# Linear attention beside a gated SwiGLU: x transposed by DMA throughout, loads split over two queues, fixed PSUM banks

## The chip, the cores and the metric

The kernel runs on one core of one Trainium2 chip. The metric is device time in microseconds, lower is better. A core has five engines that run side by side: TensorE (PE: matmuls; its weight loads are listed as PEld), VectorE (DVE), ScalarE (ACT), GpSimd (POOL) and SyncE (SP). Transfers are issued by SP and by ACT, each in its own program order, and are carried out by 16 DMA engines.

## The reference

The input x has 2,048 tokens of width 512. Two blocks work on the same x, and a gate of each token mixes them:

```python
x = A_x
g = _sigmoid((x * gate_w).sum(-1, keepdims=True))
a = _A_ref(x, A_wqkv, A_wo)       # linear attention, 32 heads of 16
b = _B_ref(x, B_w1, B_w3, B_w2)   # (silu(x @ w1) * (x @ w3)) @ w2, hidden width 1376
return g * a + (1 - g) * b
```

In the attention block q, k and v are the three thirds of `x @ wqkv`; `phi(t) = where(t > 0, t + 1, exp(t)) + 1e-6` is applied to q and k. For each head `kv` is the sum over tokens of the outer product of phi(k) and v, and `z` the sum of phi(k); the output is `phi(q) @ kv / (phi(q) . z + 1e-6)`, multiplied by `wo`. Nothing is causal. All data are bf16.

## The kernel before

**Stages.** The 2,048 tokens are 16 token tiles of 128 (index t), the width 512 is 4 pieces of 128 (index kc). A matmul contracts over the 128 partitions, so x is needed twice in SBUF: `xT` (width on the partitions, tokens along the row) as operand of every projection and of the SwiGLU, and natural `xN` (tokens on the partitions).

- *First stage (L296 to L337).* For each t a `k_step` (four matmuls with `wk` into a PSUM bank, then `phi`: an exponential on ACT, two operations on DVE, result `pk`), a `q_step` (the same with `wq`, result kept in `pq`), and a `g_step`, which adds `xN` transposed times `pk` into four PSUM banks that stay allotted for all 16 tiles. v is never formed: the sums over tokens of x times phi(k) are multiplied by `wv` later (`kv_step`). POOL adds up `pk` in `zacc`.
- *Second stage (L398 to L419).* For each of four blocks of 512 tokens ten `glu_step`s (eight matmuls each with `w1` and `w3`), with `kv_step`, `m2_step`, the denominators and the remaining 96 hidden columns (`rem_step`) set between them, and four `out_step`s, which combine both blocks and store.

**What sets the order.** The order of the program text is the order on each engine; no planner moves anything. Waits between engines and on transfers are put in from the tiles that are read and written. In the order of instructions each transfer also waits for the landing of the eighth transfer before it, counted over both queues.

**The loads (L86 to L115).** SP issues `xN` tile 0, `wk` 1, `wk` 2, `xN` tile 2, then `wq` whole, then transposing transfers (`transpose=True`) that write `xT` from x in HBM for tokens 512 to 1,023 (four, one for each kc, L96), `xN` tiles 4 to 7 (L97), transposing transfers for tokens 1,024 to 2,047 (four, L99), the rest of `xN`, and all remaining weights. ACT issues `wk` 0, `xN` tile 1, `wk` 3 and `xN` tile 3, and then the table load for its exponential.

**The first 512 tokens.** The first four token tiles of `xT` are not loaded: `transpose_step` (L191) transposes natural x on TensorE by means of an identity matrix (`ident`, built on POOL, L70), into PSUM tiles `xTp`, and DVE copies them to `xT` (L197). Before this come ten small matmuls on a zeroed tile (`warm_step`, L199), and two more behind the first transposes; their result is used nowhere. The text at L298 to L308 weaves transposes, `k_step` 0 and 1 together; then k2, k3, q0, g0, q1, g1, and from t = 2 on q(t), k(t+2), g(t).

**PSUM.** There are eight banks. Products (k, q, gate, up, the remainder) rotate over a pool of four (`mm_tile`). The other four are first those of `xTp`, then the accumulators of `g_step`, then a rotation for the a and b products (`ab_tile`), as pools that are opened one after the other.

The code that the change touches:

Of the kernel before, what the change touches and what calls it, by code (L numbers as in the profile page):

```python
# [16 lines left out]
def kernel(  # L17
# [17 lines left out]
    nc = tc.nc  # L35
    P = nc.NUM_PARTITIONS
# [5 lines left out]
    KC = D // P  # L42
# [6 lines left out]
    F0 = FC * P  # L49
    HPC = P // Dh  # L50
    NR = 2 * FR + 1
    NPE = TPB

    x2d = A_x.flatten_outer_dims()
    out2d = out.flatten_outer_dims()
    x_r = x2d.rearrange("s (kc d) -> s kc d", d=P)
# [7 lines left out]
    psum = ctx.enter_context(tc.tile_pool(name="psum", bufs=4, space=bass.MemoryType.PSUM))  # L64
# [4 lines left out]
    ident = consts.tile([P, P], BF16, name="ident")  # L69
    make_identity(nc, ident[:])  # L70


    xN = consts.tile([P, NT, D], BF16, name="xN")
# [6 lines left out]
    w3 = consts.tile([P, KC, F0], BF16, name="w3")  # L80
    w2 = consts.tile([P, FC + 1, D], BF16, name="w2")
    xT = consts.tile([P, KC, S], BF16, name="xT")
    dq = nc.sync
    aq = nc.scalar
    k_cols = slice(D, 2 * D)
    dq.dma_start(out=xN[:, 0, :], in_=x_t[:, 0, :])  # L86
    aq.dma_start(out=wk[:, 0, :], in_=wqkv_r[:, 0, k_cols])
    dq.dma_start(out=wk[:, 1, :], in_=wqkv_r[:, 1, k_cols])  # L88
    aq.dma_start(out=xN[:, 1, :], in_=x_t[:, 1, :])
    dq.dma_start(out=wk[:, 2, :], in_=wqkv_r[:, 2, k_cols])  # L90
    aq.dma_start(out=wk[:, 3, :], in_=wqkv_r[:, 3, k_cols])
    dq.dma_start(out=xN[:, 2, :], in_=x_t[:, 2, :])
    aq.dma_start(out=xN[:, 3, :], in_=x_t[:, 3, :])
    dq.dma_start(out=wq[:], in_=wqkv_r[:, :, 0:D])
    for kc in range(KC):
        dq.dma_start(out=xT[:, kc, TB : 2 * TB], in_=x_r[TB : 2 * TB, kc, :], transpose=True)  # L96
    dq.dma_start(out=xN[:, 4:8, :], in_=x_t[:, 4:8, :])  # L97
    for kc in range(KC):
        dq.dma_start(out=xT[:, kc, 2 * TB : S], in_=x_r[2 * TB : S, kc, :], transpose=True)  # L99
# [50 lines left out]
    def project(t, w, name, between=None):  # L150
        ts = slice(t * P, (t + 1) * P)
        ps = mm_tile(name + "_ps")
        for kc in range(KC):
            nc.tensor.matmul(  # L154
                ps[:], lhsT=xT[:, kc, ts], rhs=w[:, kc, :],
                start=(kc == 0), stop=(kc == KC - 1),
            )
            if kc == 1 and between is not None:
                between()
        return ps  # L160

    def phi(ps, dst, name):
# [20 lines left out]
            )  # L183

    def k_step(t):
        k_phi(t, project(t, wk, "k"))

    def q_step(t):
        phi(project(t, wq, "q"), pq[:, t, :], "q")

    def transpose_step(t, pool):  # L191
        ps = pool.tile([P, KC, P], BF16, tag="xTp", name="xTp")
        for kc in range(KC):
            nc.tensor.transpose(  # L194
                out=ps[:, kc, :], in_=xN[:, t, kc * P : (kc + 1) * P], identity=ident[:]
            )
        nc.vector.tensor_copy(out=xT[:, :, t * P : (t + 1) * P], in_=ps[:])  # L197

    def warm_step(ps, n):  # L199
        for _ in range(n):  # L200
            nc.tensor.matmul(
                ps[:, 0:256], lhsT=warm[:, 0:P], rhs=warm[:], start=True, stop=True
            )


    def rem_step(tb):

        hr = hrem[tb % 2]
        for half in range(2):
            ps = psum.tile([P, 2, 256], FP32, tag="mm", name="r_ps")  # L210
# [26 lines left out]
        dq.dma_start(  # L237
            out=hT[tb][:, FC, :].rearrange("p (tt q) -> p tt q", q=P),
            in_=hr[:].rearrange("p tt f -> p (tt f)"), transpose=True,
        )  # L240

    def glu_step(tb, fc):
        fs = slice(fc * P, (fc + 1) * P)
        tok = slice(tb * TB, (tb + 1) * TB)
        g_ps = mm_tile("gate_ps")
# [5 lines left out]
        u_ps = mm_tile("up_ps")  # L251
# [43 lines left out]

    hT = {}  # L296
    hT[0] = work.tile([P, FC + 1, TB], BF16, tag="hT", name="hT")
    with tc.tile_pool(name="psumT", bufs=NPE, space=bass.MemoryType.PSUM) as psumT:  # L298
# [10 lines left out]
    with tc.tile_pool(name="psumG", bufs=KC, space=bass.MemoryType.PSUM) as psumG:  # L309
        g_acc = [psumG.tile([P, D], FP32, tag="G", name=f"g_acc{kc}") for kc in range(KC)]  # L310

        def g_step(t):
            for kc in range(KC):
                nc.tensor.matmul(  # L314
                    g_acc[kc][:], lhsT=xN[:, t, kc * P : (kc + 1) * P], rhs=pk[t][:],
                    start=(t == 0), stop=(t == NT - 1),
                )

        k_step(2)
        k_step(3)  # L320
        q_step(0)
        g_step(0)
        q_step(1)
        g_step(1)
        for t in range(2, NT):
            q_step(t)
            if t + 2 < NT:
                k_step(t + 2)
            g_step(t)
        z_ps = mm_tile("z_ps")  # L330
        nc.tensor.matmul(z_ps[:], lhsT=ones[:], rhs=zaccb[:], start=True, stop=True)
        nc.vector.tensor_copy(out=zb[:], in_=z_ps[:])  # L332
        for kc in range(KC):
            if kc % 2 == 0:
                nc.vector.tensor_copy(out=Gsb[:, kc, :], in_=g_acc[kc][:])
            else:
                nc.scalar.activation(out=Gsb[:, kc, :], in_=g_acc[kc][:], func=ACT.Copy)  # L337

    psum2 = ctx.enter_context(tc.tile_pool(name="psum2", bufs=4, space=bass.MemoryType.PSUM))

    def ab_tile(name):
        return psum2.tile([P, D], FP32, tag="ab", name=name)

    def kv_step():
        kv_ps = psum2.tile([P, KC, P], FP32, tag="ab", name="kv_ps")
        for c in range(KC):
            cs = slice(c * P, (c + 1) * P)
            for kc in range(KC):
# [2 lines left out]
                    start=(kc == 0), stop=(kc == KC - 1),  # L351
                )
        nc.vector.tensor_tensor(
            out=kvT[:], in0=kv_ps[:],
            in1=bmask[:].rearrange("p h d -> p (h d)")[:, None, :].to_broadcast([P, KC, P]),
            op=ALU.mult,
        )

    def m2_step():
        for c in range(KC):  # L360
            ps = ab_tile("m2_ps")
# [6 lines left out]
    def out_step(tb, tt):  # L368
        t = tb * TPB + tt
        ts = slice(t * P, (t + 1) * P)  # L370
        tl = slice(tt * P, (tt + 1) * P)
        a_ps = ab_tile("a_ps")
# [9 lines left out]
        w = D // pieces  # L382
        for i in range(pieces):
            cs = slice(i * w, (i + 1) * w)
            b_ps = ab_tile("b_ps")
# [64 lines left out]
```

## Time and profile before

| what | value |
|---|---|
| median of 3 runs | 181.54 us (180.47 to 181.67) |
| the profiled execution | 182.96 us |
| its span | 181.2 us |
| PE busy | 176.6 us, 97% of the span |
| DVE busy | 103.2 us, 57% |
| ACT busy | 61.8 us, 34% |
| POOL busy | 55.3 us, 31% |
| read from HBM | 8.42 MB |
| first stage, by the first gate_ps matmul | until 49.86 us |

The time is that of the whole program on the device; the span is the part that the profile shows, from its first to its last instruction, and all places in time below are us from the span's start. A group's busy time can hide in that of another engine: what sets the end is read from the chain of work that ended last, which is followed back from the last instruction. Matmuls are pipelined, so a matmul's own duration (379 ns for 512 columns) is longer than the distance from one to the next.

### The profile page before, as it was taken

To read this page: it belongs to the slowest core of one execution; us is meant where nothing else is said; L and a number is where in the kernel's file an instruction comes from. 1 tells how busy PE (TensorE), PEld (TensorE's weight loads), DVE (VectorE), ACT (ScalarE), POOL (GpSimd) and SP (SyncE) were. 2 spreads that over 40 slices of the span, in tenths; PEclk is the share of its full clock that TensorE was granted. 3 is DMA by queue.
4 is the path that set the end of the run, shared out by engine and by line. 5 is a ranking of instruction groups with operands and counts; after the bars stand their busy time and mean duration, and the time that the engine had idled before them with its cause. 6 is when DMAs were issued, how large, how long until landed. Compare 5 with 4: busy or idle time off the path is not lost.

```text
span 181.2 us, 2439 instructions
## 1 busy us (share of the span) xinstructions
PE 176.6 (97%) x876; PEld 84.8 (47%) x876; DVE 103.2 (57%) x196; ACT 61.8 (34%) x110; POOL 55.3 (31%) x60
## 2 busy tenths in 40 slices
PE   7999999999999999999999999999999999999993
PEld 4444444444445464454444455444445544444452
DVE  1279889889899773466534345653434565343222
ACT  2153443544472533132233313223331322333130
POOL 5035335453558540247400024640003442000000
PEclk9999999999999999999999999999999999999999
DMA  5999999900001203032300003430000342000011
GB/s 149 241 244 204 252 353 398 368 3 0 5 0 29 58 0 62 29 87 66 81 0 4 0 29 87 73 77 0 0 0 29 89 81 67 0 0 0 29 40 50
DMA packets 28108, 14.88 MB, mean 82 GB/s; under 512 B 19424, under 2 KB 27072, under 8 KB 28096
## 3 DMA queue, kind: packets, MB, share of 16 engines
q1 hardware_dynamic: 27520, 14.20, 29.7%
q10 hardware_dynamic: 576, 0.52, 0.9%
q8 instruction: 7, 0.11, 0.3%
q14 instruction: 5, 0.04, 0.1%
HBM read 8.42 MB, written 2.10 MB: 58 GB/s over the span
## 4 chain that ended last, share of the span: by engine, by line
PE 95%; DMA 3%; SPq 0%; DVE 0%; issue 0%
PE b_ps L388 21%; PE gate_ps L247 19%; PE up_ps L253 19%; PE k_ps L154 8%; PE a_ps L374 8%; PE g_acc L314 8%; PE q_ps L154 8%; PE r_ps L214 3%; DMA wk<-in_A_wqkv_dram 3%; PE kv_ps L349 0%; PE m_ps L362 0%; PE xTp L194 0%; DVE o L392 0%; SPq L88 0%; SPq L86 0%
## 5 line engine op out<-in xcount | busy, mean ns | idle before, releaser
L259 DVE TENSOR_TENSOR hT<-up_ps,sg 128x512 bf16<-128x512 f32 x40 | 27.2, 680 | 30.9 <-PE up_ps L253 30.9
L253 PE MATMUL up_ps<-xT,w 128*128 128x512 bf16 x160 | 41.1, 379 | 0.0
L247 PE MATMUL gate_ps<-xT,w 128*128 128x512 bf16 x160 | 41.1, 379 | 0.0
L388 PE MATMUL b_ps<-w,hT 128*128 128x512 bf16 (+3 forms) x187 | 40.7, 367 | 0.0
L258 ACT ACTIVATE sg<-gate_ps 128x512 bf16<-128x512 f32 x40 | 23.9, 597 | 46.9 <-PE gate_ps L247 46.9
L281 POOL TENSOR_TENSOR pqs<-pq,rden 128x512 bf16<-128x512 bf16 x16 | 16.9, 1055 | 65.0 <-issue 60.0
L392 DVE SCALAR_TENSOR_TENSOR o<-b_ps,omg_all,aga 128x512 bf16<-128x512 f32 (+1 forms) x17 | 12.2, 720 | 28.4 <-PE b_ps L388 28.4
L388 PEld LDWEIGHTS <-hT 128*128 128x128 bf16 (+1 forms) x187 | 18.3, 98 | 19.9
L253 PEld LDWEIGHTS <-w 128*128 128x128 bf16 x160 | 15.7, 98 | 18.9
L247 PEld LDWEIGHTS <-w 128*128 128x128 bf16 x160 | 15.6, 98 | 18.4
L181 POOL TENSOR_TENSOR zacc<-zacc,pk 128x512 f32<-128x512 f32 x14 | 16.3, 1162 | 18.4 <-DVE pk L169 18.2
L379 ACT ACTIVATE aga<-a_ps,g_all 128x512 f32<-128x512 f32 x16 | 11.0, 687 | 28.9 <-PE a_ps L374 28.9
L154 PEld LDWEIGHTS <-xT 128*128 128x128 bf16 x128 | 12.8, 101 | 15.6 <-issue 1.2
L266 POOL TENSOR_TENSOR pr<-pq,zb 128x512 f32<-128x512 bf16 x16 | 18.4, 1154 | 2.5 <-DVE zb L332 2.5
L154 PE MATMUL k_ps<-wk,xT 128*128 128x512 bf16 x64 | 18.4, 414 | 0.3 <-DMA wk<-in_A_wqkv_dram 0.2
L314 PE MATMUL g_acc<-pk,xN 128*128 128x512 bf16 x64 | 16.4, 379 | 0.0
L374 PE MATMUL a_ps<-M,pqT 128*128 128x512 bf16 x64 | 16.4, 378 | 0.0
L154 PE MATMUL q_ps<-wq,xT 128*128 128x512 bf16 x64 | 16.4, 379 | 0.0
L164 ACT ACTIVATE eq<-q_ps 128x512 bf16<-128x512 f32 x16 | 9.6, 598 | 17.2 <-PE q_ps L154 16.1
L164 ACT ACTIVATE ek<-k_ps 128x512 bf16<-128x512 f32 x16 | 9.6, 598 | 9.3 <-PE k_ps L154 9.3
L169 DVE SCALAR_TENSOR_TENSOR pk<-k_ps,emk 128x512 bf16<-128x512 f32 x16 | 11.1, 692 | 1.6
L169 DVE SCALAR_TENSOR_TENSOR pq<-q_ps,emq 128x512 bf16<-128x512 f32 x16 | 11.1, 692 | 0.5
(47 smaller groups left out, 96.7 us busy)
## 6 DMA issues: line engine op xcount, KB each, us to landing
w<-in_B_w_dram SPq DMA_DIRECT2D x3, 1280.0 KB, 8.5
out_dram<-o SPq DMA_DIRECT2D x15, 128.0 KB, 1.9
xN<-in_A_x_dram SPq DMA_DIRECT2D x3, 512.0 KB, 5.6
wq<-in_A_wqkv_dram SPq DMA_DIRECT2D x1, 512.0 KB, 5.3
wv<-in_A_wqkv_dram SPq DMA_DIRECT2D x1, 512.0 KB, 9.0
wo<-in_A_wo_dram SPq DMA_DIRECT2D x1, 512.0 KB, 9.5
wk<-in_A_wqkv_dram ACTq DMA_DIRECT2D x2, 128.0 KB, 3.8
xN<-in_A_x_dram SPq DMA_DIRECT2D x2, 128.0 KB, 3.7
```

What stands on the lines that cost most here:

```text
L154: nc.tensor.matmul(ps[:], lhsT=xT[:, kc, ts], rhs=w[:, kc, :], start=(kc == 0), stop=(kc == KC - 1),)
L164: nc.scalar.activation(out=e[:], in_=ps[:], func=ACT.Exp)
L169: nc.vector.scalar_tensor_tensor(out=dst, in0=ps[:], scalar=0.0, in1=em[:], op0=ALU.max, op1=ALU.add)
L247: nc.tensor.matmul(g_ps[:], lhsT=w1[:, kc, fs], rhs=xT[:, kc, tok], start=(kc == 0), stop=(kc == KC - 1),)
L253: nc.tensor.matmul(u_ps[:], lhsT=w3[:, kc, fs], rhs=xT[:, kc, tok], start=(kc == 0), stop=(kc == KC - 1),)
L258: nc.scalar.activation(out=sg[:], in_=g_ps[:], func=ACT.Silu)
L259: nc.vector.tensor_tensor(out=hT[tb][:, fc, :], in0=u_ps[:], in1=sg[:], op=ALU.mult)
L266: nc.gpsimd.tensor_tensor(out=pr[t][:], in0=pq[:, t, :], in1=zb[:], op=ALU.mult)
L281: nc.gpsimd.tensor_tensor(out=pqs[:].rearrange("p (h d) -> p h d", d=Dh), in0=pq[:, t, :].rearrange("p (h d) -> p h d", d=Dh), in1=rden[t] ...
L314: nc.tensor.matmul(g_acc[kc][:], lhsT=xN[:, t, kc * P : (kc + 1) * P], rhs=pk[t][:], start=(t == 0), stop=(t == NT - 1),)
L374: nc.tensor.matmul(a_ps[:], lhsT=pqT[:, c, ts], rhs=M2[:, c, :], start=(c == 0), stop=(c == KC - 1),)
L388: nc.tensor.matmul(b_ps[:, 0:w], lhsT=hT[tb][:n, fc, tl], rhs=w2[:n, fc, cs], start=(fc == 0), stop=(fc == FC),)
```

## The change

All of `xT` now comes from transposing transfers, one for each token tile of 128 with all four kc pieces in it, and all of them on SP, from its first instruction on; the natural tiles 4 to 7, 8 to 11 and 12 to 15 stand behind the transposes 5, 8 and 11. ACT issues `wk` (pieces 0, 1, then 2 and 3 as one), `wq` in two halves and natural tiles 0 to 3 as one transfer, and then runs an exponential on one column of the zeroed tile. `ident`, `transpose_step` and the weaving are gone; twelve of the small matmuls stand ahead of k0. The first steps run in the order k0, k1, q0, k2, q1, g0, k3, g1 and from t = 2 on as before. The PSUM pools become eight tiles that are allotted once: products rotate over banks 4 to 7, the accumulators and then the a and b products use banks 0 to 3.

```diff
-    dq.dma_start(out=xN[:, 0, :], in_=x_t[:, 0, :])
+    def load_xT(t):
+        ts = slice(t * P, (t + 1) * P)
+        dq.dma_start(out=xT[:, :, ts], in_=x2d[ts, :], transpose=True)
+
+    def load_xN(q, t0, t1):
+        q.dma_start(out=xN[:, t0:t1, :], in_=x_t[:, t0:t1, :])
+
     aq.dma_start(out=wk[:, 0, :], in_=wqkv_r[:, 0, k_cols])
-    dq.dma_start(out=wk[:, 1, :], in_=wqkv_r[:, 1, k_cols])
-    aq.dma_start(out=xN[:, 1, :], in_=x_t[:, 1, :])
-    dq.dma_start(out=wk[:, 2, :], in_=wqkv_r[:, 2, k_cols])
-    aq.dma_start(out=wk[:, 3, :], in_=wqkv_r[:, 3, k_cols])
-    dq.dma_start(out=xN[:, 2, :], in_=x_t[:, 2, :])
-    aq.dma_start(out=xN[:, 3, :], in_=x_t[:, 3, :])
-    dq.dma_start(out=wq[:], in_=wqkv_r[:, :, 0:D])
-    for kc in range(KC):
-        dq.dma_start(out=xT[:, kc, TB : 2 * TB], in_=x_r[TB : 2 * TB, kc, :], transpose=True)
-    dq.dma_start(out=xN[:, 4:8, :], in_=x_t[:, 4:8, :])
-    for kc in range(KC):
-        dq.dma_start(out=xT[:, kc, 2 * TB : S], in_=x_r[2 * TB : S, kc, :], transpose=True)
-    dq.dma_start(out=xN[:, 8:12, :], in_=x_t[:, 8:12, :])
-    dq.dma_start(out=xN[:, 12:16, :], in_=x_t[:, 12:16, :])
+    aq.dma_start(out=wk[:, 1, :], in_=wqkv_r[:, 1, k_cols])
+    aq.dma_start(out=wk[:, 2:4, :], in_=wqkv_r[:, 2:4, k_cols])
+    aq.dma_start(out=wq[:, 0:2, :], in_=wqkv_r[:, 0:2, 0:D])
+    aq.dma_start(out=wq[:, 2:4, :], in_=wqkv_r[:, 2:4, 0:D])
+    load_xN(aq, 0, 4)
+    nc.scalar.activation(out=act_pre[:], in_=warm[:, 0:1], func=ACT.Exp)
+    for t in range(NT):
+        load_xT(t)
+        if t in (5, 8, 11):
+            i = {5: 4, 8: 8, 11: 12}[t]
+            load_xN(dq, i, i + 4)
...
-    def mm_tile(name):
-        return psum.tile([P, D], FP32, tag="mm", name=name)
+    bank = [psum.tile([P, D], FP32, name=f"bank{i}") for i in range(8)]
+    turn = {"mm": 0, "ab": 0}
+
+    def mm_tile():
+        turn["mm"] += 1
+        return bank[4 + (turn["mm"] - 1) % 4]
+
+    def ab_tile():
+        turn["ab"] += 1
+        return bank[(turn["ab"] - 1) % 4]
...
-        w_ps = mm_tile("warm_ps")
-        warm_step(w_ps, 10)
-        transpose_step(0, psumT)
-        warm_step(w_ps, 2)
-        k0 = project(0, wk, "k", between=lambda: transpose_step(1, psumT))
-        transpose_step(2, psumT)
-        k1 = project(1, wk, "k")
-        transpose_step(3, psumT)
-        k_phi(0, k0)
-        k_phi(1, k1)
...
-        k_step(2)
-        k_step(3)
-        q_step(0)
-        g_step(0)
-        q_step(1)
-        g_step(1)
...
+    for _ in range(12):
+        nc.tensor.matmul(
+            bank[3][:, 0:256], lhsT=warm[:, 0:P], rhs=warm[:], start=True, stop=True
+        )
+    k_step(0)
+    k_step(1)
+    q_step(0)
+    k_step(2)
+    q_step(1)
+    g_step(0)
+    k_step(3)
+    g_step(1)
+    for t in range(2, NT):
+        q_step(t)
+        if t + 2 < NT:
+            k_step(t + 2)
+        g_step(t)
```

More of the change, by code (lines that the diff above doesn't have):

```diff
@@ L6 @@
 from concourse._compat import with_exitstack
-from concourse.masks import make_identity
 ACT = mybir.ActivationFunctionType
@@ L51 @@
     NR = 2 * FR + 1
-    NPE = TPB
     x2d = A_x.flatten_outer_dims()
     out2d = out.flatten_outer_dims()
-    x_r = x2d.rearrange("s (kc d) -> s kc d", d=P)
     x_t = x2d.rearrange("(t p) d -> p t d", p=P)
@@ L63 @@
     work = ctx.enter_context(tc.tile_pool(name="work", bufs=2))
-    psum = ctx.enter_context(tc.tile_pool(name="psum", bufs=4, space=bass.MemoryType.PSUM))
+    psum = ctx.enter_context(tc.tile_pool(name="psum", bufs=1, space=bass.MemoryType.PSUM))
     ctx.enter_context(tc.manual_schedule())
@@ L68 @@
     nc.vector.memset(warm[:], 0.0)
-    ident = consts.tile([P, P], BF16, name="ident")
-    make_identity(nc, ident[:])
     xN = consts.tile([P, NT, D], BF16, name="xN")
@@ L82 @@
     xT = consts.tile([P, KC, S], BF16, name="xT")
+    act_pre = consts.tile([P, 1], BF16, name="act_pre")
     dq = nc.sync
@@ L144, with project @@
     th_all = consts.tile([P, NT], FP32, name="th_all")
-    def mm_tile(name):
-        return psum.tile([P, D], FP32, tag="mm", name=name)
-    def project(t, w, name, between=None):
-        ts = slice(t * P, (t + 1) * P)
-        ps = mm_tile(name + "_ps")
+    bank = [psum.tile([P, D], FP32, name=f"bank{i}") for i in range(8)]
[6 more added lines that the diff above has]
+        return bank[(turn["ab"] - 1) % 4]
+    def project(t, w):
+        ps = mm_tile()
         for kc in range(KC):
             nc.tensor.matmul(
-                ps[:], lhsT=xT[:, kc, ts], rhs=w[:, kc, :],
+                ps[:], lhsT=xT[:, kc, t * P : (t + 1) * P], rhs=w[:, kc, :],
                 start=(kc == 0), stop=(kc == KC - 1),
             )
-            if kc == 1 and between is not None:
-                between()
         return ps
@@ L185, in k_step, with g_step @@
     def k_step(t):
-        k_phi(t, project(t, wk, "k"))
+        k_phi(t, project(t, wk))
     def q_step(t):
-        phi(project(t, wq, "q"), pq[:, t, :], "q")
-    def transpose_step(t, pool):
-        ps = pool.tile([P, KC, P], BF16, tag="xTp", name="xTp")
+        phi(project(t, wq), pq[:, t, :], "q")
+    def g_step(t):
         for kc in range(KC):
[L194 to L200, printed above, removed]
             nc.tensor.matmul(
-                ps[:, 0:256], lhsT=warm[:, 0:P], rhs=warm[:], start=True, stop=True
+                bank[kc][:], lhsT=xN[:, t, kc * P : (kc + 1) * P], rhs=pk[t][:],
+                start=(t == 0), stop=(t == NT - 1),
             )
@@ L209, in rem_step @@
         for half in range(2):
-            ps = psum.tile([P, 2, 256], FP32, tag="mm", name="r_ps")
+            ps = mm_tile()[:].rearrange("p (j n) -> p j n", j=2)
             for j in range(2):
@@ L244, in glu_step @@
         tok = slice(tb * TB, (tb + 1) * TB)
-        g_ps = mm_tile("gate_ps")
+        g_ps = mm_tile()
         for kc in range(KC):
@@ L250, in glu_step @@
             )
-        u_ps = mm_tile("up_ps")
+        u_ps = mm_tile()
         for kc in range(KC):
@@ L297 @@
     hT[0] = work.tile([P, FC + 1, TB], BF16, tag="hT", name="hT")
-    with tc.tile_pool(name="psumT", bufs=NPE, space=bass.MemoryType.PSUM) as psumT:
-        w_ps = mm_tile("warm_ps")
-        warm_step(w_ps, 10)
-        transpose_step(0, psumT)
-        warm_step(w_ps, 2)
-        k0 = project(0, wk, "k", between=lambda: transpose_step(1, psumT))
-        transpose_step(2, psumT)
-        k1 = project(1, wk, "k")
-        transpose_step(3, psumT)
-        k_phi(0, k0)
-        k_phi(1, k1)
@@ L309 @@
[L309 to L317, printed above, removed]
-        k_step(2)
-        k_step(3)
-        q_step(0)
-        g_step(0)
-        q_step(1)
-        g_step(1)
[L325 to L337, printed above, removed]
@@ L339 @@
-    psum2 = ctx.enter_context(tc.tile_pool(name="psum2", bufs=4, space=bass.MemoryType.PSUM))
-    def ab_tile(name):
-        return psum2.tile([P, D], FP32, tag="ab", name=name)
+    for _ in range(12):
[15 more added lines that the diff above has]
+        g_step(t)
@@ L344, in kv_step @@
+    z_ps = mm_tile()
+    nc.tensor.matmul(z_ps[:], lhsT=ones[:], rhs=zaccb[:], start=True, stop=True)
+    nc.vector.tensor_copy(out=zb[:], in_=z_ps[:])
+    for kc in range(KC):
+        if kc % 2 == 0:
+            nc.vector.tensor_copy(out=Gsb[:, kc, :], in_=bank[kc][:])
+        else:
+            nc.scalar.activation(out=Gsb[:, kc, :], in_=bank[kc][:], func=ACT.Copy)
     def kv_step():
-        kv_ps = psum2.tile([P, KC, P], FP32, tag="ab", name="kv_ps")
+        kv_ps = ab_tile()[:].rearrange("p (c q) -> p c q", q=P)
@@ L353, in kv_step @@
         nc.vector.tensor_tensor(
-            out=kvT[:], in0=kv_ps[:],
+            out=kvT[:], in0=kv_ps,
             in1=bmask[:].rearrange("p h d -> p (h d)")[:, None, :].to_broadcast([P, KC, P]),
@@ L360, in m2_step @@
         for c in range(KC):
-            ps = ab_tile("m2_ps")
+            ps = ab_tile()
             nc.tensor.matmul(ps[:], lhsT=kvT[:, c, :], rhs=wo[:, c, :], start=True, stop=True)
@@ L371, in out_step @@
         tl = slice(tt * P, (tt + 1) * P)
-        a_ps = ab_tile("a_ps")
+        a_ps = ab_tile()
         for c in range(KC):
@@ L384, in out_step @@
             cs = slice(i * w, (i + 1) * w)
-            b_ps = ab_tile("b_ps")
+            b_ps = ab_tile()
             for fc in range(FC + 1):
```

## The prediction

> **What bounds the kernel now.** I read the page's chain that ended last first, then the same chain over the first 30 us, the DMA issues, and the SP queue in order of time.
>
> ```profile
> PE 95%; DMA 3%; SPq 0%; DVE 0%; issue 0%
> ```
>
> ```profile
> xN<-in_A_x_dram SPq DMA_DIRECT2D x3, 512.0 KB, 5.6
> wq<-in_A_wqkv_dram SPq DMA_DIRECT2D x1, 512.0 KB, 5.3
> ...
> pqT<-pqs SPq DMA_TRANSPOSE x16, 2.4
> ...
> xT<-in_A_x_dram SPq DMA_TRANSPOSE x8, 4.1
> ```
>
> TensorE carries 95% of the chain and one load the rest. So only a gap on PE, or PE work removed, moves the end; what other engines gain is worth nothing unless PE waits for them. The second fence is the DMA view; its last two figures are size and median us from issue to landing (a transpose has no size shown).
>
> The chain at the start (start us, us, what):
>
> ```profile
> 1.74 4.54 DMA wk<-in_A_wqkv_dram
> 6.28 0.04 issue
> 6.32 1.01 PE k_ps L154 x2
> 7.33 0.43 PE xTp L194 x4
> 7.76 1.71 PE k_ps L154 x4
> 9.46 0.43 PE xTp L194 x4
> 9.89 1.93 PE k_ps L154 x8
> 11.82 0.86 PE q_ps L154 x4
> 12.68 0.86 PE g_acc L314 x4
> ```
>
> Here the reader sees three things. The third quarter of wk lands at 6.28 and starts the chain. Four 512-column matmuls take 1.71 us at 7.76 but 0.86 us from 11.82 on: PE runs at half pace until about 10.1 (eight at 9.89 take 1.93, so one or two are slow). The granted-clock column says 1.00 throughout, so the pace has to be read from the matmuls. Two groups of transposes stand in the chain after 6.32, 0.43 us each. From 11.82 to 49.86, where gate_ps begins, PE has no gap.
>
> A "step" below is one k, q or g step (4 matmuls). **The yardstick:** before, six steps (k0 to k3, q0, g0) are through at 12.68 + 0.86 = 13.55 us. In the changed order the first six are k0, k1, q0, k2, q1, g0; the seventh and eighth are again the same set. So the change is worth the time at which its g0 ends, less 13.55, if nothing stalls later.
>
> **Part 1, removed.** Sixteen TensorE transposes and four DVE copies (425 ns each). On the chain the transposes are 2 x 0.43 = 0.86 us; the others ran while PE waited for wk. The DVE copies lay on a DVE that waited for them anyway: no gain by themselves.
>
> **Part 2, the transposing DMAs.** The SP queue in order of time prices the issues:
>
> ```profile
> 3.70 0.39 SPq L94 DMA_DIRECT2D wq<-in_A_wqkv_dram  x1
> 4.13 5.15 SPq L96 DMA_TRANSPOSE xT<-in_A_x_dram  x4
> 9.33 0.58 SPq L97 DMA_DIRECT2D xN<-in_A_x_dram  x1
> 9.96 5.88 SPq L99 DMA_TRANSPOSE xT<-in_A_x_dram  x4
> ```
>
> An issue takes some 1.25 us whether it carries 512 or 1,024 tokens (medians 1.256 and 1.297), and the 128-token pqT form takes 1.19. So SP goes from 8 transposing issues to 16, one token tile each 1.25 us: tile t is issued at about 0.8 + 1.25t, plus 0.55 for each natural load between. Landing took 3.0 to 5.4 us, median 4.1. PE takes a new tile each 2.6 us, so later tiles get ever more lead (tile 4: issued 5.8, landed by 11.2, needed about 16). Everything behind on SP moves: 16 x 1.25 + 3 x 0.55 ends at 22.5 instead of 17.06, 5.4 us later. w1 is then issued near 26 and, with the longest landing of a large weight (12.2), is in by 38; gate_ps needs it at 49.9. wv lands near 37 for 55.0, w2 near 42 for 71.1. Cost nothing, covered by 12 us and more.
>
> Natural tiles 4 to 7: issued near 8.3, in by 14.6 at 6.3 us; g4 comes near 22. Nothing.
>
> **Part 3, the ACT queue.** It now issues wk0, wk1, wk2:4 (quarters 2 and 3), wq0:2, wq2:4, xN0:4 (natural x, token tiles 0 to 3), and behind these stand the table load (1.28 us) and every exponential. The order of instructions shows that a DMA waits until the eighth DMA before it, over both queues, has landed: wq2:4 waits for xT1, xN0:4 for xT2. This is the new wait.
>
> - wk2:4: the old third quarter, issued at 1.74 (this one at about 1.73), landed at 6.28. Less lies ahead of it (two quarters on its own queue, about two transposes beside it). Bounds 5.0 (the 2.8 to 3.0 us of the first loads, on 256 KB) and 6.3; I take 6.0.
> - xT2 is issued at 3.3, lands by the median at 7.4 (6.3 to 8.7). xN0:4, 512 KB: 4.0, 5.6 and 6.3 us in three natural loads, 5.3 for wq. wq is nearest, as it went out into the same crowd. Landed at 7.4 + 5.3 = 12.7 (10.3 to 15.0).
> - wq2:4 goes out when xT1 lands, 2.05 + 3.5 = 5.5, and takes 2.7 (128 KB) to 5.3 (512 KB): 8.2 to 10.8, I take 9.5.
> - ACT is free for k0 at 7.4 + 0.45 issue + 1.28 table + 0.1 = 9.2; exponential 0.60, DVE 0.28 + 0.69: pk0 at 10.8. q1 wants its PSUM bank, and g0 wants it as operand.
>
> PE then: k0's second half 6.0 to 6.85, k1 to 8.56 (1.71), q0's first half to 9.41, its second waits to 9.5 and ends near 10.3, k2 11.2, q1 12.1. g0 could start at 12.1, but its weights are natural x, landed 12.7. Four matmuls in a row of their own take 1.03: 13.73 against 13.55. **Sum: +0.2 us.** The 0.86 saved and the earlier wk are handed back by waiting for the natural tiles, which earlier PE transposes needed at once and which now come last.
>
> A check by bytes: in half-us windows the old kernel has moved 2.13 MB by 11.0, which is wk, wq, xN0:4 (12 units of 131 KB), almost all of four transposed units, and table and code. The new one needs those 12, xT0 to xT5 and part of xN4:8: 18 to 20 units and table and code (0.15 MB), 0.38 to 0.64 MB more: at the 310 GB/s of 11 to 13 us by 12.2 to 13.1, at the 201 GB/s of 7.5 to 10.5 (transposes in flight) by 12.9 to 14.2. Both ends go into the range. A lone transpose (pqT) is seen here, columns from the left us, PE, weights, DVE, ACT, POOL, clock, DMA share, GB/s:
>
> ```profile
> 152.00:152.50 0.50, 0.50 (x4) 0.26 (x3) 0.07 (x1) 0.33 (x1) 0.00 (x0) 1.00 0.44 88
> 152.50:153.00 0.50, 0.50 (x4) 0.20 (x3) 0.00 (x0) 0.27 (x1) 0.00 (x0) 1.00 0.88 174
> ```
>
> It fills all DMA engines for 0.66 us (0.22 + 0.44) per 131 KB: 198 GB/s. The Trainium skill, "DMA: Bandwidth & Descriptors", section Latency and other measured facts, gives 261 GB/s for a DMA transpose; by that estimate six tiles cost 3.0 us of the engines and not 4.0, and natural x would land up to 1 us sooner. The row here is slower than the page.
>
> **Part 4, banks and the rest.** Products rotate over four banks and accumulators or a/b over four, as the pools did: from the eighth step on, each step still takes the bank of the one four before it. Nothing either way. The identity on POOL goes (nobody waits), the early exponential only fixes where the table load stands. From 13.7 on all rows repeat. DVE, busy 0.88 to 0.97 of the time from 10 us on, has no more to do than before.
>
> The profiled execution took 182.96 us, span 181.2 and 1.8 around it; with +0.2 it would be 183.2. The median of the runs, 181.54, lies 0.8% below it; applied there: **181.7 us**.
>
> **Rivals.**
>
> A. *PE, not natural x, is last.* xN0:4 lands before PE gets there (xT2 after 3.0 us, then 4.0: 10.3). g0 starts at 12.1, or with wk2:4 at 5.0 and no break at 11.5: 0.6 to 1.2 us earlier than 12.68. 180.3 to 180.9. For it: the faster windows (361 GB/s at 2.5 to 3.5). Against: between 7 and 10 us the DMA share reads above 1 in five of six half-us windows, transposes in flight, at 130 to 313 GB/s: the load is limited by the DMA engines there.
>
> B. *The slow pace lasts longer.* Before, PE was busy without a break from 6.32 until the pace doubled at 10.1, 3.8 us; it did not double after the broken stretch 1.1 to 6.3. If the break at wq2:4 (up to 10) starts this anew, PE stays slow to 13.8: k1 8.56, q0 10.4, k2 12.1, q1 13.8, g0 ends 14.8, +1.3: 182.8. The Trainium skill, "TensorE: Matmul & The Clock Gate", Part 1, has a free-running window of about 3.4 us that must be busy before full clock; by that page a miss costs an estimated 1.7 us. The 3.8 us here agrees with it roughly.
>
> C. *Slower: the ACT queue is held by landing transposes.* If transposes among copies land late (xT2 after 5.4: 8.7) and natural x at 6.3, g0 starts at 15.0: +2.5 us, 184.0; at the 128 GB/s seen in 8 to 9 us, the 1.15 MB that are left at 7.5 (2.64 less 1.50) take 8.9 us, 16.4 and +3.9, 185.4. ACT starts later as well (pk0 12.1, q1 stalls), but that lies inside. It decides from a landing at about 14.3, +1.8. For it: those two windows, and a queue that stands still behind each wait. Against: SP offers a 0.66 us transpose only each 1.25 us.
>
> **How the numbers follow.** Chances: forecast 0.40 (181.2 to 182.4), A 0.25, B 0.20, C 0.15. A measurement of this kernel tells about 1% (1.8 us) from no change: faster means under 179.7, slower over 183.4. A's 0.25 holds 0.08 past its best (the pace doubling early as well): faster. Slower: C and B's late part, 0.18. Same 0.74. The range reaches from A's low end to C's first price: 180.2 to 184.0.
>
> **What would show it.** Right: xTp gone, chain of the start going through the xN load of the ACT queue, g0 starting near 12.7, gate_ps at 50 +- 0.5, and matmul rows after that unchanged. A: g0 near 12 with no DMA in the chain but wk. B: 0.43 us matmuls after 11 us. C: a PE gap of over 1.5 us before g0, ACT idle before its table load. I am wrong altogether if a gap stands after 16 us: then the weights pushed back on SP, or the banks, cost what I put at nothing.

## The result, and the profile after

The changed kernel takes **187.08 us** (median of 4 runs, 186.54 to 187.45) against 181.41 beside it: a ratio of 1.0308, 95% interval 1.0283 to 1.0333. It is 5.7 us slower; the prediction was 181.7 us, range 180.2 to 184.0, with 0.18 on slower. Times here and below are medians of fast runs; the one slow run of a variant, 186.41 us of the kernel with the copies behind, is also the run that its trace shows.

The page's chain that ended last, after:

```profile
PE 91%; DMA 5%; SPq 1%; issue 1%; DVE 0%
```

PE's share of the chain fell from 95% to 91%, and two loads stand in it in place of one. The chain at the start (start us, us, what) shows which:

```profile
2.14 5.92 DMA xT<-in_A_x_dram
8.06 0.02 issue
8.08 4.02 DMA wq<-in_A_wqkv_dram
12.10 0.04 issue
12.14 4.11 PE bank L161 x10
16.24 0.86 PE bank L198 x4
```

The second transposing transfer (xT1, issued at 2.14) lands at 8.06. At 8.08 starts the load of wq's second half, which waited for it (by the order of instructions, xT1 is the eighth transfer before it), and lands at 12.10. Ten matmuls then take 4.11 us; at the pace of the next line (4 in 0.86) they would take 2.15. g0 ends at 17.11.

PE in order of time, after (start us, us, engine, line, what, idle before and what ended it):

```profile
6.02 1.01 PE L161 MATMUL bank<-wk,xT 128*128 128x512 bf16 x2 [0.34 <-DMA wk<-in_A_wqkv_dram]
8.10 1.89 PE L161 MATMUL bank<-wk,xT 128*128 128x512 bf16 x4 [1.07 <-DMA xT<-in_A_x_dram]
9.78 1.06 PE L161 MATMUL bank<-wq,xT 128*128 128x512 bf16 x2
12.14 1.01 PE L161 MATMUL bank<-wq,xT 128*128 128x512 bf16 x2 [1.29 <-DMA wq<-in_A_wqkv_dram]
12.94 1.91 PE L161 MATMUL bank<-wk,xT 128*128 128x512 bf16 x4
14.65 1.59 PE L161 MATMUL bank<-wq,xT 128*128 128x512 bf16 x4
16.08 1.03 PE L198 MATMUL bank<-pk,xN 128*128 128x512 bf16 x4
```

Read it in two ways. The brackets are the waits: for xT1 ahead of k1, and for wq in the middle of q0. The durations are the pace: four matmuls take 1.9 us up to k2 (0.43 from one to the next, and the last one's tail), 1.59 in q1, and 1.03 (0.22 from one to the next) only from 16 us on.

ACT in order of time, after:

```profile
2.20 0.67 ACTq L93 DMA_DIRECT2D wq<-in_A_wqkv_dram  x1
8.08 0.38 ACTq L94 DMA_DIRECT2D wq<-in_A_wqkv_dram  x1
8.49 0.48 ACTq L88 DMA_DIRECT2D xN<-in_A_x_dram  x1
9.01 1.28 ACT L96 ACT_TABLE_LOAD   x1 [9.01 <-DMA xT<-in_A_x_dram]
```

ACT stands still from 2.87 to 8.08, on the wait for xT1.

From g0 on nothing is new: gate_ps starts at 53.44 instead of 49.86, which is 3.58 later, as g0 ended 3.56 later (17.11 for 13.55), and the profiled spans differ by 3.4 (184.6 and 181.2). But the medians differ by 5.7. So the first question was where the other 2.2 us are.

### The profile page after: what moved, and what is told of

Read it like the earlier page. It is cut to its first block, busy times and chain, and to the rows that moved or that the text cites. A ratio compares the mean times of both kernels' runs of the same rounds, so it can differ in the third digit from the quotient of the medians.

```text
span 184.6 us, 2395 instructions
## 1 busy us (share of the span) xinstructions
PE 176.2 (95%) x844; PEld 83.5 (45%) x860; DVE 102.4 (55%) x192; ACT 61.8 (33%) x111; POOL 54.9 (30%) x58
## 4 chain that ended last, share of the span: by engine, by line
PE 91%; DMA 5%; SPq 1%; issue 1%; DVE 0%
PE bank L366 21%; PE bank L245 19%; PE bank L251 18%; PE bank L161 15%; PE bank L198 8%; PE bank L352 7%; DMA xT<-in_A_x_dram 3%; PE bank L212 3%; DMA wq<-in_A_wqkv_dram 2%; SPq L85 1%; PE bank L327 0%; PE bank L340 0%; DVE o L370 0%; PE bank L314 0%
## 5 line engine op out<-in xcount | busy, mean ns | idle before, releaser
L257 DVE TENSOR_TENSOR hT<-bank,sg 128x512 bf16<-128x512 f32 x40 | 27.2, 681 | 30.9 <-PE bank L251 27.8
L245 PE MATMUL bank<-xT,w 128*128 128x512 bf16 x159 | 41.0, 379 | 0.2
L366 PE MATMUL bank<-w,hT 128*128 128x512 bf16 (+3 forms) x186 | 40.6, 367 | 0.1
L251 PE MATMUL bank<-xT,w 128*128 128x512 bf16 x153 | 40.2, 379 | 0.2
L256 ACT ACTIVATE sg<-bank 128x512 bf16<-128x512 f32 x40 | 23.9, 597 | 46.9 <-PE bank L245 46.9
L370 DVE SCALAR_TENSOR_TENSOR o<-bank,omg_all,aga 128x512 bf16<-128x512 f32 (+1 forms) x17 | 12.2, 719 | 28.4 <-PE bank L366 28.4
L161 PE MATMUL bank<-wk,xT 128*128 128x512 bf16 x62 | 18.9, 427 | 2.2 <-DMA xT<-in_A_x_dram 1.9
L161 PE MATMUL bank<-wq,xT 128*128 128x512 bf16 x63 | 17.8, 405 | 1.3 <-DMA wq<-in_A_wqkv_dram 1.3
L198 PE MATMUL bank<-pk,xN 128*128 128x512 bf16 x63 | 16.4, 379 | 0.2
L352 PE MATMUL bank<-M,pqT 128*128 128x512 bf16 x61 | 16.3, 378 | 0.2
L174 DVE SCALAR_TENSOR_TENSOR pk<-bank,emk 128x512 bf16<-128x512 f32 x16 | 11.1, 692 | 2.0 <-PE bank L161 0.5
```

The lines of the kernel that those rows point to most:

```text
L161: nc.tensor.matmul(ps[:], lhsT=xT[:, kc, t * P : (t + 1) * P], rhs=w[:, kc, :], start=(kc == 0), stop=(kc == KC - 1),)
L198: nc.tensor.matmul(bank[kc][:], lhsT=xN[:, t, kc * P : (kc + 1) * P], rhs=pk[t][:], start=(t == 0), stop=(t == NT - 1),)
L245: nc.tensor.matmul(g_ps[:], lhsT=w1[:, kc, fs], rhs=xT[:, kc, tok], start=(kc == 0), stop=(kc == KC - 1),)
L251: nc.tensor.matmul(u_ps[:], lhsT=w3[:, kc, fs], rhs=xT[:, kc, tok], start=(kc == 0), stop=(kc == KC - 1),)
L256: nc.scalar.activation(out=sg[:], in_=g_ps[:], func=ACT.Silu)
L257: nc.vector.tensor_tensor(out=hT[tb][:, fc, :], in0=u_ps[:], in1=sg[:], op=ALU.mult)
```

## The experiments

Theory at this point: the loss lies in the first 16 us and has three parts, a landing (xT1), a wait on the ACT queue (wq's second half behind xT1) and the slow matmul pace, which the gaps prolong. Rivals: the banks, the 128-token transposes or the later weights cost something; or the DMA engines are simply full.

**The kernel before again** (no edit).

> The kernel before, unchanged, with a trace of its own. The median moved by 5.7 us, the two profiled spans by 3.4 (181.2 to 184.6). Theory: the profiled execution of before was a late one, in which the matmul pace doubled only at 10.1 us; other executions double earlier, have spans near 179.5, and this trace shows the pace doubling before 9 us. Rival: spans are again near 181.2 and the 2.2 us lie outside the span, so that the changed kernel loses time before its first or after its last instruction.

181.41 us, the same time. Its trace is another than that of the page before: the span is 179.6, and the ten spans of this set are 179.1 to 179.7. The chain at its start:

```profile
2.19 4.82 DMA xN<-in_A_x_dram
7.01 0.05 issue
7.05 0.40 PE xTp L194 x4
7.45 0.86 PE k_ps L154 x4
8.31 0.22 PE xTp L194 x4
8.54 1.73 PE k_ps L154 x8
10.26 0.86 PE q_ps L154 x4
11.13 0.86 PE g_acc L314 x4
```

k1's four matmuls take 0.86 us here and took 1.71 on the page before; the transposes take 0.22 for 0.43. The pace had doubled by 6.3 us, and g0 ends at 11.99 instead of 13.55. **The page before shows a rare execution** (of 24 spans of the kernel before in the last set two more are at 181.0 and 181.2, nearly all others at 178.7 to 180.1). Against the usual one the changed kernel's spans (median 184.7) are 5.2 longer than this set's 179.45, which leaves 0.4 of the 5.7 to what lies around the span. The theory held.

**Small matmuls in TensorE's gaps.** `fill(n)` issues n matmuls on a zeroed tile into a bank that nothing reads; the table in `project` gives how many follow which matmul of a step.

```diff
...
-    k_step(0)
+    fill(3)
+    k_phi(0, project(0, wk, {1: 2, 3: 6}))
     k_step(1)
-    q_step(0)
+    phi(project(0, wq, {1: 7}), pq[:, 0, :], "q")
```

> The changed kernel with 18 small matmuls on the zeroed tile set into the three places where TensorE waits for a load (ahead of k0, within and behind it, and in the middle of q0); loads untouched. Theory: about half of the loss is the slow matmul pace up to 15.4 us, which the gaps prolong; with the gaps filled the pace doubles by about 10, the loads still hold q0 until 12.1, and g0 ends near 15.2 instead of 17.1: span near 182.7, time near 185. Rival (the loads alone set the start, the pace hides in the waits): g0 ends at 17 as before, span 184.6.

185.33 us, 1.75 less than the changed kernel. PE in order of time:

```profile
4.62 0.60 PE L167 MATMUL bank<-wk,xT 128*128 128x512 bf16 x2 [0.22 <-DMA xT<-in_A_x_dram]
8.29 1.04 PE L167 MATMUL bank<-wk,xT 128*128 128x512 bf16 x4 [0.81 <-DMA xT<-in_A_x_dram]
11.71 0.59 PE L167 MATMUL bank<-wq,xT 128*128 128x512 bf16 x2 [1.19 <-DMA wq<-in_A_wqkv_dram]
14.86 1.04 PE L205 MATMUL bank<-pk,xN 128*128 128x512 bf16 x4 [0.84 <-DMA xN<-in_A_x_dram]
```

Here the first two k0 matmuls already run at full pace at 4.6 and no later ones are slow; the waits for xT1 and wq stay (8.29 and 11.71 for 8.10 and 12.14), and a wait for natural x appears at 14.86, where PE now arrives first. g0 ends at 15.9. So filling the gaps gets back 1.75 us of the 5.7, in runs that don't overlap (184.15 to 185.93 against 186.54 to 187.45), and what is left goes with the loads. That the small matmuls are what doubled the pace so early isn't shown: two traces below without them have the first k0 matmuls at full pace at 4.2 and 4.3 (256 KB beside, copies behind), and one with them is slow until about 10 (wk as two transfers, filled).

**The old start with all else changed.** The loads of the first 512 tokens, the TensorE transposes and the order of the first eight steps as before; the fixed banks, one transposing transfer for each later token tile and the weights behind them as changed.

```diff
-    for t in range(NT):
+    for t in range(TPB, NT):
         load_xT(t)
...
+    k0 = project(0, wk, between=lambda: transpose_step(1))
```

> The changed kernel with the start of the kernel before: its loads for the first 512 tokens and wk, wq, the TensorE transposes and the order of its first eight steps. What stays changed: one transposing transfer for each of the token tiles 4 to 15 with four pieces in it, the place of the later natural tiles, the weights 4 us later on SP, the fixed banks. Theory: all of the loss lies in the first 512 tokens, so the time is that of before, 181.4 within 0.6. Rival: the banks, the weights or the 128-token transposes cost something later: over 183.

181.09 us, ratio 0.9985 (0.9969 to 1.0001). All of the loss is in the start; the banks, the later transposes of 128 tokens and the later weights cost nothing that shows, as predicted.

**wq as one transfer**, so that no ACT load waits for a transpose.

```diff
-    aq.dma_start(out=wq[:, 0:2, :], in_=wqkv_r[:, 0:2, 0:D])
-    aq.dma_start(out=wq[:, 2:4, :], in_=wqkv_r[:, 2:4, 0:D])
+    aq.dma_start(out=wq[:], in_=wqkv_r[:, :, 0:D])
```

> The changed kernel with wq as one transfer. By the order of instructions no ACT load then waits for a transposing transfer: wq goes out near 2.2 and natural x, which now waits for wk1 only, near 4.5. Theory (the waits on the ACT queue are the cost): q0 does not wait for wq, its 1.5 us gap goes, the pace doubles near 12, g0 ends near 14.5 instead of 17.1: span near 182, time 184.4. Rival (the DMA engines are the limit, and earlier copies only crowd the transposes): xT1 and xT2 land later than 8.1 and 8.2, k1 waits longer, and g0 ends at 16.5 or later.

185.88 us: 1.2 less, half of what the theory wanted. wq no longer holds q0, but it lies in front of the transposes: wq (issued 2.2) lands at 9.3 and xT1 at 9.57, 1.5 later than in the changed kernel. g0 ends at 15.91. Each side was half right: the wait goes, and later landings take back more than half of it.

**What does a transpose wait for?** Three kernels vary what lies beside the first transposes: the copies put behind them on SP, rows of 2 KB, rows of 512 bytes. The fourth adds small matmuls to the first of them. The lines below are, in turn, from the copies behind xT3, from the 2 KB rows (wq and wk of one quarter in one transfer, four such), and from the 512-byte rows (each weight as two transfers of half rows).

```diff
+        if t == 3:
+            dq.dma_start(out=wq[:], in_=wqkv_r[:, :, 0:D])
+            load_xN(dq, 0, 4)
...
+    aq.dma_start(out=wqk[:, 0, :], in_=wqkv_r[:, 0, 0 : 2 * D])
...
+    halves(wk, 0, 4, D)
+    halves(wq, 0, 4, 0)
```

> The changed kernel with wq (one transfer) and natural tiles 0 to 3 taken from ACT and put on SP behind xT3, so that only wk lies beside the first transposes. Theory (the DMA engines take one packet of each queue in turn, 1 KB of a copy against 256 bytes of a transpose, so that xT1 lands only when the copies of the other queue have run out: 8.06 us behind wk and half of wq, 9.57 behind wk and all of wq): with 512 KB on ACT xT0 and wk end together near 5, xT1 lands by 5.8 and k1 does not wait; g0 ends near 14.5, time near 184. Rival (engines share by bytes, or a transpose from HBM is slow by itself): xT1 lands at 7.5 or later as before.

> The changed kernel with wk and wq side by side in one tile, loaded by four transfers whose rows are 2 KB long instead of 1 KB; the same bytes. Theory (turns by packet): xT0, 32 packets on each engine, lands when ACT has moved about 32 packets of 2 KB, or all it has: 5.2 us or later instead of 4.6, and xT1 after 8. Rival (shares by bytes): xT0 lands at 4.6 or earlier, since longer rows only make the copies cheaper.

> The changed kernel with wk and wq each loaded as two column halves, rows of 512 bytes instead of 1 KB; the same bytes in twice the packets, which is the worse form for a copy alone. Theory (turns by packet): the transposes gain, xT0 lands near 3.9 instead of 4.6 and xT1 near 5.5 instead of 8.06, while wk ends no later than 6.3; the time falls below the changed kernel's 187.1, to 184 to 185.5. Rival (shares by bytes, the engines limited by the count of packets): xT1 lands at 8 or later and the time is 187 or more.

> Copies behind the transposes as in the first kernel of this set, and small matmuls in TensorE's gaps as in the earlier one, together. Theory: the two causes are separate, the order of the loads and the slow matmul pace that its gaps prolong; together g0 ends near 12.5 and the time is near that of before, 181.3 to 182.3. Rival (something else costs, too): it stays above 183.

| kernel | on ACT before 2.9 us | xT0 lands | xT1 lands | time, us |
|---|---|---|---|---|
| changed | 768 KB, 4 transfers | 4.6 | 8.06 | 187.08 |
| wq as one | 1,024 KB, 4 | 4.45 | 9.57 | 185.88 |
| copies behind | 512 KB, 3 | 4.25 | 6.2 | 185.01 |
| 2 KB rows | 768 KB, 3 | 5.2 | 6.5 | 186.18 |
| 512-byte rows | 768 KB, 3 | 5.96 | 7.5 | 182.83 |

Landings vary from trace to trace: with small matmuls added and the same loads, the copies behind have xT1 at 5.5 instead of 6.2, the changed kernel at 8.25 instead of 8.06.

With the copies behind, k1 starts at 6.24 and waits only 0.22, as forecast. But wq is now late, and its wait shows what a gap costs twice:

```profile
6.24 1.04 PE L161 MATMUL bank<-wk,xT 128*128 128x512 bf16 x4 [0.22 <-DMA xT<-in_A_x_dram]
10.73 1.87 PE L161 MATMUL bank<-wq,xT 128*128 128x512 bf16 x4 [3.46 <-DMA wq<-in_A_wqkv_dram]
12.39 1.83 PE L161 MATMUL bank<-wk,xT 128*128 128x512 bf16 x4
```

At 6.24 four matmuls took 1.04, after 3.46 us of idling they take 1.87: the pace has fallen back. With small matmuls added (186.11 us) this gap stays, 3.00 us, since none of them stands in it, and k2 behind it is slow as well (1.91 at 12.31); the forecast of 181.3 to 182.3 failed.

The theory of turns by packet fell. The 2 KB rows agree with it for xT0, but not for xT1 (6.5, forecast after 8); with 512-byte rows xT0 lands at 5.96, forecast 3.9. The Trainium skill, "DMA: Bandwidth & Descriptors", section Queues, rings and completion order, says that a DMA engine goes round its queues and changes at packet boundaries, with some 9 to 17 descriptors to a packet. The theory took a single row for a packet, which is not what the page says, so these two runs refute the theory and leave the page's rule untested. What holds in all five: xT1 lands 0.2 to 0.8 us behind the last copy that ACT issued by 2.9 us. It follows wq's first half (8.06 behind 7.7; with 512-byte rows 7.5 behind 7.2), all of wq (9.57 behind 9.3), wk's last part where nothing else is there (6.2 behind 5.4), wq's and wk's third piece with 2 KB rows (6.5 behind 5.9). That is a pattern, not a mechanism.

The surprise is the 512-byte rows: 4.25 us faster than the changed kernel. They have four transfers ahead of natural x instead of five. Each transfer waits for the eighth one before it, and by the order of instructions this shifts the count: wq's second half then waits for xT0, not for xT1, and went out at 5.98 instead of 8.08. (The 2 KB rows have four, too, and their last piece goes out at 5.25; but it holds the last quarter of wk, so k0 waits for it until 9.65.)

**One ACT transfer less.** The count alone, with bytes, rows and order as in the changed kernel; and the same with the gaps filled.

```diff
-    aq.dma_start(out=wk[:, 0, :], in_=wqkv_r[:, 0, k_cols])
-    aq.dma_start(out=wk[:, 1, :], in_=wqkv_r[:, 1, k_cols])
+    aq.dma_start(out=wk[:, 0:2, :], in_=wqkv_r[:, 0:2, k_cols])
```

> The changed kernel with the first two quarters of wk as one transfer. The bytes, rows and order are the same, only there is one ACT transfer less ahead of wq's second half, and by the order of instructions this half now waits for xT0 instead of xT1 (landed 4.6 and 8.06). Theory (of the loss, the wait on the ACT queue is one part by itself): xT1 still lands near 8, since the same 768 KB go out ahead of it, but wq's second half is issued near 4.7 instead of 8.08 and lands by 10 instead of 12.1; q0 has no break, g0 ends near 14.5 instead of 17.1, time 184 to 185. Rival (the engines are full, an earlier issue only moves the crowd): it lands at 11.5 or later, time over 186.5.

182.65 us, ratio to before 1.0075 (1.0050 to 1.0101): **4.4 of the 5.7 us are back**. The chain at its start and ACT in order of time:

```profile
0.80 4.78 DMA xT<-in_A_x_dram
5.58 0.05 issue
5.63 6.79 PE bank L160 x20
12.42 0.86 PE bank L197 x4
```

```profile
5.60 0.38 ACTq L93 DMA_DIRECT2D wq<-in_A_wqkv_dram  x1
6.02 0.48 ACTq L88 DMA_DIRECT2D xN<-in_A_x_dram  x1
6.53 1.28 ACT L95 ACT_TABLE_LOAD   x1 [6.53 <-DMA xT<-in_A_x_dram]
```

xT0 lands later than in the changed kernel (5.58 for 4.6), but then PE has no break at all: twenty matmuls in a row, the pace doubles within q0, g0 ends at 13.28. wq's second half lands at 9.3, and natural x, which goes out right behind it, at 11.9. Better than forecast, and for a second reason: xT1 landed at 6.8, where theory had it unchanged near 8.

> The kernel just above with the small matmuls in TensorE's gaps ahead of, within and behind k0 and in q0. Theory: the two parts add up; the pace doubles by 6, g0 ends near 13, and the time is 182 to 183. Rival (they are one and the same loss): no faster than the kernel above.

183.43 us, no faster than without (the runs overlap, 182.40 to 184.34 against 182.24 to 183.07). The parts don't add up: where no load is late any more, the small matmuls stand in the way. The trace, of the slowest of the four runs, has 15 of them in the chain, 2.5 us, eight at the slow pace.

**A fourth dose beside xT1.**

```diff
+        if t == 1:
+            dq.dma_start(out=wk[:, 2:4, :], in_=wqkv_r[:, 2:4, k_cols])
```

> Only the first half of wk (256 KB) is on ACT; the other half is on SP behind xT1, wq and natural tiles 0 to 3 on SP behind xT3. A fourth dose for the landing of xT1: behind 1,024 KB of copies it landed at 9.57 us, behind 768 KB at 8.06, behind 512 KB at 6.2. Theory (a transpose lands when the bytes issued ahead of it have been moved, some 1.7 us for each 256 KB): near 4.6, not before its own issue ends at 3.4 plus some 0.8. Rival (a second transpose behind the first has a price of its own): 5.5 or later.

xT1 lands at 4.8, 0.6 behind xT0, against 4.6 forecast: no price for a transpose behind another shows. The time, 185.85, is that of a late wk and wq (1.8 and 2.7 us of waiting on PE). PE in order of time, and below it half-us windows (the clock is the third column from the right):

```profile
4.24 0.61 PE L161 MATMUL bank<-wk,xT 128*128 128x512 bf16 x2 [0.38 <-DMA xT<-in_A_x_dram]
6.63 1.94 PE L161 MATMUL bank<-wk,xT 128*128 128x512 bf16 x6 [1.79 <-DMA wk<-in_A_wqkv_dram]
11.28 1.87 PE L161 MATMUL bank<-wq,xT 128*128 128x512 bf16 x4 [2.71 <-DMA wq<-in_A_wqkv_dram]
```

```profile
7.00:7.50 0.50, 0.50 (x4) 0.19 (x2) 0.00 (x0) 0.24 (x1) 0.00 (x0) 0.97 0.75 169
7.50:8.00 0.50, 0.50 (x3) 0.20 (x2) 0.11 (x1) 0.36 (x1) 0.00 (x0) 0.50 0.51 32
8.00:8.50 0.50, 0.50 (x2) 0.09 (x1) 0.47 (x2) 0.00 (x0) 0.00 (x0) 0.50 0.80 90
```

The clock falls to 0.50 at 7.5, in the middle of k0 and k1 and ahead of the 2.71 us wait, so that wait is not what slowed q0. The longest wait before it is 1.79 us.

**Which of the two: the wait, or the earlier landing?** One kernel gives the wait back to the kernel with wk as two transfers (wq's first half as two quarters); one keeps the lone first quarter of wk and merges the other three (the last line).

```diff
+    aq.dma_start(out=wq[:, 0, :], in_=wqkv_r[:, 0, 0:D])
+    aq.dma_start(out=wq[:, 1, :], in_=wqkv_r[:, 1, 0:D])
...
+    aq.dma_start(out=wk[:, 1:4, :], in_=wqkv_r[:, 1:4, k_cols])
```

> wk as two transfers (as in the 182.65 us kernel), but wq's first half as two quarters, so that ACT has five transfers ahead of natural x again, wq's second half waits for xT1 and natural x for xT2, as in the changed kernel. Theory (the wait carries most of it): xT1 lands near 7 and wq's second half is issued then, lands near 11, q0 has a gap of 1 us or more, the slow pace lasts longer, time 184.5 to 186.5. Rival (the lone first quarter and the slump behind it carry it): 183.3 or less.

> wk as its first quarter alone and the other three as one transfer: four ACT transfers ahead of natural x, and wq's second half waits for xT0. Theory (the wait carries most of it): wq's second half is issued near 4.7 and lands by 10, time 182.3 to 183.5, wherever xT1 lands. Rival (the lone first quarter lets xT0 land at 4.6, and the slump of the DMA engines behind it, 54 to 156 GB/s between 5.0 and 6.5, carries it): xT1 at 7.8 or later and time over 184.5.

With the wait back: 184.53 us, 1.9 more. wq's second half goes out at 6.82, behind xT1, and natural x at 8.34, behind xT2; natural x is what PE then waits for, at 14.14. Its chain:

```profile
3.44 4.88 DMA xT<-in_A_x_dram
8.32 0.02 issue
8.34 5.80 DMA xN<-in_A_x_dram
14.14 0.05 issue
14.19 1.04 PE bank L198 x4
```

Lone first quarter without the wait: 182.29 us (1.0075, 1.0041 to 1.0110), xT0 at 5.54 and xT1 at 6.7. So the waits, for both loads, are worth 1.9 of the 4.4 us, and the lone quarter has no part in it. The other 2.5 are what remains, without a run of their own: the landing of xT1 at 6.8 instead of 8.06, with no gap ahead of k1 (1.07 in the changed kernel), and a pace that doubles at 9 to 10 instead of after 15. In half-us windows (last two columns: DMA share, GB/s), changed kernel first, the lone quarter without the wait second:

```profile
5.00:5.50 0.50, 0.50 (x2) 0.15 (x1) 0.00 (x0) 0.00 (x0) 0.00 (x0) 1.00 0.48 54
5.50:6.00 0.50, 0.18 (x1) 0.00 (x0) 0.00 (x0) 0.00 (x0) 0.00 (x0) 1.00 1.16 156
6.00:6.50 0.50, 0.48 (x2) 0.10 (x1) 0.00 (x0) 0.00 (x0) 0.00 (x0) 1.00 1.03 122
```

```profile
5.00:5.50 0.50, 0.00 (x0) 0.00 (x0) 0.00 (x0) 0.00 (x0) 0.00 (x0) 1.00 1.13 301
5.50:6.00 0.50, 0.41 (x2) 0.14 (x3) 0.00 (x0) 0.00 (x0) 0.00 (x0) 1.00 1.39 225
6.00:6.50 0.50, 0.50 (x3) 0.22 (x2) 0.00 (x0) 0.01 (x1) 0.00 (x0) 1.00 1.30 261
```

The same 768 KB lie ahead of xT1 in both, issued by 2.9 us in four transfers or in three; with four, the engines move 54 to 156 GB/s for 1.5 us, with three 225 to 301 here and 163 to 219 with wk as two halves. The other two kernels that issued four copies of 1 KB rows by 2.9 us show such a slump too: 90, 187 and 195 GB/s with the gaps filled, 96, 97 and 171 with wq as one. The kernel with the wait given back has four as well, but its fourth went out only at 3.88, when wk's first half had landed: 254, 259 and then 100 GB/s, and xT1 at 6.8. A single slow window tells nothing by itself: the lone quarter without the wait has one of 89 GB/s from 3.0 to 3.5. **Why four go worse than three stays open.**

**Faster than both?** The old start with natural tile 1 behind all of wk, and the old start with wk as two transfers (the lines shown).

```diff
+    aq.dma_start(out=wk[:, 0:2, :], in_=wqkv_r[:, 0:2, k_cols])
+    dq.dma_start(out=wk[:, 2:4, :], in_=wqkv_r[:, 2:4, k_cols])
+    aq.dma_start(out=xN[:, 1, :], in_=x_t[:, 1, :])
+    dq.dma_start(out=xN[:, 2:4, :], in_=x_t[:, 2:4, :])
```

> The kernel with the old start (TensorE transposes of tiles 0 to 3, fixed banks, 128-token transposes for the rest), with natural tile 1 behind all four quarters of wk instead of ahead of two of them. Theory (loads land in the order in which they are issued, k0's second half waits for wk's last quarters at 6.1): these land about 0.4 earlier, time 180.6 to 181.0, below the kernel before. Rival (natural tile 1 or 2 takes over as the last): 181.3 or more.

> The kernel with the old start and wk as two transfers, wk's first half on ACT and the second on SP behind natural tile 0, then natural tile 1 on ACT and 2 and 3 as one on SP. Theory (fewer transfers, wk complete sooner: 5.5 instead of 6.1): 180.4 to 180.9, below the kernel before. Rival (natural tile 1 or 2 is last instead): 181.2 or more.

The first: 181.30 us, 1.0021 (0.9987 to 1.0056), no gain; natural tile 1 lands at 6.10 and PE waits 0.42 us for it. That trace is of an execution of 183.20 us, one of three late ones among twelve, so the price of the gap can't be read from it. The second: **180.76 us, 0.9963 (0.9938 to 0.9987)**, 0.4 us faster than the kernel before. wk is complete by 5.5, and all following steps run without a wait; g0 ends at 11.02.

## Why the prediction was wrong

**The yardstick.** 13.55 us for six steps came from an execution whose pace doubled at 10.1; the usual one has 11.99. That is 1.56 of the 5.7 us. The numbers to see it were in the table: 182.96 for the profiled execution, outside the 180.47 to 181.67 of the runs. I noted the difference, and laid a gain measured on the late execution on the median of the usual ones.

**Part 1, the 0.86 us of transposes.** Gone as forecast (in the usual execution they are 0.62), and of no use: they had stood in a chain almost without gaps, and the new one has gaps.

**Part 2.** The issues cost what was forecast (six in 7.82 us, 1.30 each), w1 went out at 25.96 (forecast near 26), and no gap on PE stands after 16 us. Right.

**Part 3, where the sum failed.** "wk2:4 at 6.0" held (6.02). "xT1 at 2.05 + 3.5 = 5.5" did not: it took 5.9 us, beyond the 3.0 to 5.4 of the rows, and landed at 8.06. In the rows the transposes went out from 4.13 on, when ACT had issued its last copy (2.67); here ACT issued 768 KB by 2.9 us, around the first two, and in the runs with 256 to 1,024 KB beside it xT1 lands later with each dose (4.8, 6.2, 8.06, 9.57). It is not the bytes alone: the same 768 KB in three transfers have it at 6.5 to 7.5. I had priced those copies for the natural tiles, in the check by bytes, and not for xT1. From this follow k1 at 8.10 (in the sum 6.85) and wq's second half issued at 8.08 (5.5) and landed at 12.10 (9.5). The sum also had the full pace from about 10 on; k2 and most of q1 were still slow, and the ten matmuls from 12.14 on took 4.11 us. Natural x, which the sum had last at 12.7, landed at 13.7, and PE got there only at 16.1. So g0 ended at 17.11 instead of 13.73: 3.4 us by this part and 1.6 by the yardstick are most of the error.

**Part 4.** Banks and the rest cost nothing: shown for the time as a whole by the old start with all else changed (181.09 us).

**The rivals.** A did not occur: natural x was indeed not last, but because PE was late, not because x was early. B, the pace, told that matmuls of 0.43 us would stand after 11 us, and they did; its size was 1.3, the filled gaps give 1.75. C, the ACT queue held by landing transposes, was half right: ACT stood idle ahead of its table load, as it said, but the load that came late was wq, not natural x, and the gaps ahead of g0 were 1.07 and 1.29, not one of over 1.5. The price of its waits by runs is 1.9 us, in a kernel whose landings are otherwise good. The error was to give B and C chances as if only one could happen: both follow from a late landing, and they came together, 5.1 us over the usual start (17.11 against 11.99).

## What to carry to other kernels

Hold the profiled execution's own time against the runs before it serves as a yardstick; if it lies outside them, take a second trace. Where transfers are limited to so many in flight, count which earlier one each late one waits for: a transfer more or less ahead of it moved that wait from one transpose to another, and with the earlier landings was worth 4.4 us of 187. And price a gap on TensorE twice, once for the wait and once for the slow pace that can stand behind it.

## What the runs showed of the hardware

- The matmul pace has two levels, 0.43 and 0.22 us for 512 columns. In the first microseconds the granted-clock column reads 1.00 at both; when the pace falls back later, it reads 0.50. When the pace first doubles varies between executions of one kernel (6.3 and 10.1 us in the kernel before).
- The clock fell back at 10.6 us in the run with the copies behind, 3.3 us into a wait of 3.46, and came back 3.4 us later. In the run with 256 KB beside it fell at 7.5 us, 0.8 us after a wait of 1.79 had ended, and came back 6.8 us later, at 14.3. The Trainium skill, "TensorE: Matmul & The Clock Gate", Part 1, puts the fall behind an idle window of about 3.4 us that runs freely: the first agrees; in the second TensorE had at no time stood still for longer than 1.79 us.
- A transposing transfer of 128 tokens from HBM with little beside it lands 2.6 us after its issue begins (xT1 with 256 KB of copies), and 7.4 us after it with 1,024 KB.
- Half as long rows, 512 bytes, cost little: against wk as two transfers, with as many transfers and rows of 1 KB, wk was complete at 5.7 us for 4.9 and wq at 9.9 for 9.3, at about the same time (182.83 and 182.65 us).
